# Routed attention and a Strassen MLP on one core: rows of x turned later, conversions spread anew, VectorE in written order in the first second layer

## The chip, the core and the metric

The kernel runs on one core of a Trainium2 chip. A core has TensorE (PE, matmuls, results in PSUM), VectorE (DVE), ScalarE (ACT) and GpSimd (POOL), and SyncE (SP), which issues most DMAs here. Each engine works through its own instructions in order and waits on semaphores for the others. The metric is the device time of one execution in microseconds.

## The reference, cut to what matters

Attention with 8 heads in 4 sequences of 768 tokens: a query sees only the keys that have the same nearest centroid (of 16). Then an MLP with layer norm and a residual on rows of 512. The weights come as 64-bit floats.

```python
q_assign = np.argmax(np.einsum('bhsd,hcd->bhsc', q_n, c_n), axis=-1)
k_assign = np.argmax(np.einsum('bhsd,hcd->bhsc', k_n, c_n), axis=-1)
mask = q_assign[:, :, :, None] == k_assign[:, :, None, :]
scores = scale * np.matmul(q, k.transpose(0, 1, 3, 2))
scores = np.where(mask, scores, -1000000000.0)
scores = scores - np.max(scores, axis=-1, keepdims=True)
attn = np.exp(scores)
attn = attn / (np.sum(attn, axis=-1, keepdims=True) + 1e-09)
attn_out = np.matmul(attn, v)                       # (4, 8, 768, 64)
x = attn_out.transpose(0, 2, 1, 3).reshape(4, 768, 512)
mu = np.mean(x, axis=-1, keepdims=True)
var = np.mean((x - mu) ** 2, axis=-1, keepdims=True)
xn = (x - mu) / np.sqrt(var + 1e-06) * g_ln
ch = np.maximum(xn @ w_ch1, 0.0) @ w_ch2            # 512 -> 2048 -> 512
out = x + ch
```

## The kernel before

**Attention.** Two heads of one sequence make a pair; there are 16 pairs, n = 0 to 15, four to a sequence b. In the loop over n, TensorE does in this order: `scores` for 12 blocks of keys (a mask matmul in bf16 and the f32 matmul of q and k into one bank; ScalarE then takes the exponential), the denominators `den` of pair n - 1, `weigh` for 12 blocks (exponentials times v, into `a_ps`), and `prep_sims(n + 2)`, the similarities to the centroids. The bank of `sim_ps` is the one that the first half of `weigh` uses in the next turn of the loop, so `weigh` waits until `prep_route` (VectorE, L328) has turned the similarities out of it.

VectorE does in this order: `prep_route(n + 1)`; the reciprocal of the denominators of pair n - 2 (`finish`, part 1); `turn_pair(n + 2)`, which turns the loaded q and k blocks and asks for the next ones; `add_up(n, 0)` and `add_up(n, 1)`, which sum the exponentials of each half; `finish(n - 2, 2)`, the product of attention output and `rb` (the reciprocals, which GpSimd's DMAs have spread over all rows); `finish(n - 2, 3)`, which turns the product to rows (L513) and stores them to `x_d` with four DMAs (L516); and `weight(n, 0)`, with `weight(n, 1)` in the pairs of `TWICE`. Sequences 1 to 3 also store the product itself to `xT_d`.

`weight` converts one of 32 chunks of 128 x 512 weights from 64 to 32 bits: a 512 KB load into `raw`, three VectorE instructions in `split_weight`, two in `join_weight`, then an adding DMA of GpSimd, and the load of the chunk after next into the freed buffer. The first 16 chunks are w1, the others the 16 row blocks of w2. 22 chunks are converted in the attention, the other 10 in the first layer of sequence 0 (`within` says in which unit). Rows 7 to 15 of w2 serve as tiles for exponentials until the attention ends.

In the attention the order of TensorE, VectorE, ScalarE and GpSimd is the written one (`manual_schedule`); SP's DMAs are ordered by a planner.

**MLP.** Both layers are one level of Strassen's scheme (seven products in place of eight), in the second layer of sequences 1 to 3 two levels. The first layer runs in eight units j, with seven parts each (`first_layer`, `first_units`): four matmuls to a part, ScalarE copies or VectorE adds after it, and `w1_sums(j + 1)` on VectorE. The first unit's first copy, L853, is `p1`; TensorE's third part adds to the same bank after it. In the first layer of sequence 0 the written order holds for TensorE, VectorE and ScalarE.

The second layer of sequence 0 (`second_layer`, L934) has seven parts of three token blocks. Around it VectorE makes `hidden_sums` and `w2_sum`, the norm of sequence 1 (`norm_rows` on its rows from `x_d`, two `xr` buffers; `norm_stats`; `norm_stat_rows`, which TensorE turns and SP spreads; `norm_apply`), `x_sum` and `w1_sums`. Only TensorE's order is written there; the planner orders the rest, and moved the first w2 sums ahead into the layer before. `w2_whole` stores the converted w2 to `w_all`, four DMAs to a group of four row blocks; the planner issues a group when its blocks are ready.

Rows of x from `x_d` serve the norm's statistics in all sequences, but the residual only in sequence 0. Sequences 1 to 3 take the residual from `xT_d`.

In sequences 1 to 3, SP's order is written as well. `unit_end(b, j)` does what comes after each unit, such as statistics of the next sequence.

Of the kernel before, what the change touches and what calls it, by code (L numbers as in the profile page):

```python
# [23 lines left out]
def kernel(  # L24
# [20 lines left out]
    Q = 32  # L45
# [35 lines left out]
    TWICE = (0, 1, 3, 4, 6, 8, 9)  # L81
# [370 lines left out]
    def finish(n, part):  # L452
# [26 lines left out]
        elif part == 1:  # L479
            nc.vector.reciprocal(rdens[:, n, :], rdens[:, n, :])  # L480
            row = dram.tile([2, S], F32, tag="row", name="row")
            nc.gpsimd.dma_start(
                out=row.rearrange("j (p e) -> (j p) e", e=DE), in_=rdens[:, n, :]
            )
            if n + 1 < len(pairs):
                if n + 2 < len(pairs):
                    rb = last.tile([P, S], F32, tag="rb", name="rb", bufs=1)
                else:
                    rb = last.tile([P, 2, S], F32, tag="two", name="rb", bufs=1)[:, 0]
            else:  # L490
                rb = late["all"][:, 2]
            for j in range(2):
                nc.gpsimd.dma_start(  # L493
                    out=rb[j * D : (j + 1) * D, :],
                    in_=row[j : j + 1, :].to_broadcast([D, S]),
                )
            late[n] = rb
        elif part == 2:
            a, x = xs.pop(n), late[n]
            if b:  # L500
                nc.vector.tensor_tensor(x, a, x, ALU.mult)
                nc.sync.dma_start(out=xT_d[b][pr], in_=x)
            else:
                late[n] = norm_tiles(b)[0][:, pr, :]
                nc.vector.tensor_tensor(late[n], a, x, ALU.mult)
        else:
            x = late.pop(n)

            if n + 1 < len(pairs):
                y = last.tile([P, S], F32, tag="y", name="y")  # L510
            else:
                y = late["all"][:, 0]
            nc.vector.transpose(y, x)  # L513
            for i in range(P // Q):
                m = pr * P + i * Q
                nc.sync.dma_start(  # L516
                    out=x_d[b].rearrange("t (a r) m -> r (t a) m", r=Q)[:, :, m : m + Q],
                    in_=y[i * Q : (i + 1) * Q].rearrange("r (g f) -> r g f", f=Q),
                )
# [187 lines left out]
    with tc.manual_schedule(engines=order | {mybir.EngineType.Pool}):  # L707
# [16 lines left out]
        for n in range(len(pairs)):  # L724
# [16 lines left out]
            if n + 2 < len(pairs):  # L741
                turn_pair(n + 2)
# [12 lines left out]
            add_up(n, 1)  # L755
            for i in own[:NT]:
                weigh(i)
            if nxt:
                for piece in pieces[4:]:
                    prep_mask(n + 1, *piece)  # L760
            if n > 1 and nxt:
                finish(n - 2, 2)
                finish(n - 2, 3)
            weight(n, 0)
# [55 lines left out]
    for m in range(len(convert), NWC):  # L820
        within.setdefault((1, 2, 2, 3, 4, 4, 5, 6, 6, 7)[m - len(convert)], []).append(m)
# [98 lines left out]
    def hidden_sums(c, late):  # L920

        a11, a12, a21, a22 = [hidden[r, l, c] for r in range(2) for l in range(2)]
        if late:
            nc.vector.tensor_tensor(a12, a12, a11, ALU.subtract)
            return
        s3 = place("e")[:, c]
        hidden["s3", c] = s3
        nc.vector.tensor_tensor(s3, a11, a21, ALU.subtract)
        nc.vector.tensor_tensor(a21, a21, a22, ALU.add)
        nc.vector.tensor_tensor(a11, a21, a11, ALU.subtract)  # L930
# [10 lines left out]
    def add_rows(b, r, tt, j, bank):  # L941
# [3 lines left out]
        o = early.tile([P, MH], F32, tag="o", name="o_sb", bufs=12)  # L945
# [397 lines left out]
    with tc.manual_schedule(engines={mybir.EngineType.PE}):  # L1343
# [5 lines left out]
        relu(len(summed))  # L1349
        w2_sum(st, 1)  # L1350
        w2_keep(1, st["t", 1])
        for tt in range(TH):
            second_layer(0, tt, 1, st)
            if tt == 0:
                first_layer(0, NFH - 1, 4)
                first_layer(0, NFH - 1, 3)
        relu(len(summed))
        for c in range(NFH):
            hidden_sums(c, False)
        w2_sum(st, 2)  # L1360
        norm_load(1)
        rows_load(1, 0)
        for part in (2, 5, 6, 7, 4, 3):
            for tt in range(TH):
                second_layer(0, tt, part, st)
                if part == 6 and tt == 0:
                    norm_stat_rows(1)
            if part == 2:
                for c in range(NFH):
                    hidden_sums(c, True)  # L1370
            if part == 5:
                w2_keep(2, st["t", 2])
                w2_sum(st, 3)
                w2_keep(3, st["t", 3])
            if part == 6:
                w2_sum(st, 4)
                w2_keep(4, st["t", 2])
            if part in (2, 5):
                for tt in range(TH):
                    norm_rows(1, (0 if part == 2 else TH) + tt)  # L1380
                if part == 5:
                    norm_stats(1)
            if part == 7:
                for i in range(2):
                    for c in range(NDC):
                        norm_apply(1, i, c)
                w2_whole()
            if part == 4:
                for i in range(1, 5):
                    x_sum(1, i)  # L1390
        w1_sums(1, 0)

    with tc.manual_schedule(engines=order | {mybir.EngineType.SP}):
# [4 lines left out]
        def unit_end(b, j):  # L1398
# [6 lines left out]
            if b == 1:  # L1405
                if j == 0:
# [287 lines left out]
```

## Time and profile before

| | |
|---|---|
| median of 3 runs (lowest, highest) | 915.58 us (913.34, 917.48) |
| profiled execution: its time / its span | 914.04 us / 912.3 us |
| granted TensorE clock, mean | 0.989 |
| TensorE busy | 878.1 us (96%) |
| VectorE busy | 705.6 us (77%) |
| ScalarE busy | 402.9 us (44%) |
| GpSimd busy | 77.3 us (8%) |
| attention / first layer, sequence 0 / second layer, sequence 0 | 0 to about 338 / to about 417 / to about 492 us |

Busy times are of one profiled execution. A group's row gives its count, the busy time, the mean of one instruction in ns, and the idle time of its engine just before it with what ended it. A matmul's end is modelled and matmuls overlap, so TensorE's stalls are read from one start to the next. A window's row gives its length and, for each engine, busy us and instructions, then the granted clock, the mean busy share of the DMA engines and GB/s.

### The profile page before, as it was taken

Reading aid. Unit: us, or ns where it says so; the run is one execution under the profiler, and the core shown is the slowest. Engines: PE = TensorE matmul, PEld = TensorE weight load, DVE = VectorE, ACT = ScalarE, POOL = GpSimd, SP = SyncE. Lnnn points to the kernel's source line nnn. Section 1 sums busy time; section 2 is a strip of 40 time slices with the busy share of each in tenths; the row PEclk is TensorE's granted clock in tenths of the full one; section 3 lists DMA queues with packets and bytes.
Section 4 is the critical chain, followed back from the end, with each engine's and each line's share of the span. In section 5 each row is a group of like instructions: output and inputs, shape, how many; then the busy total and the mean of one; then the engine's idle time right before and its main releaser. Section 6 shows DMA issues by size and latency. Waiting matters only on the chain.

```text
span 912.3 us, 13180 instructions
## 1 busy us (share of the span) xinstructions
PE 878.1 (96%) x4644; PEld 576.8 (63%) x4644; DVE 705.6 (77%) x1149; ACT 402.9 (44%) x739; POOL 77.3 (8%) x143
## 2 busy tenths in 40 slices
PE   8999899998999898999999999999999999999995
PEld 5444344443444344557887556997556997556995
DVE  5899898998989897879672777896655896655774
ACT  6787678897888642332001553111553111333110
POOL 1112111211212121110000000000000000000000
PEclk9999999999999998999999999999999999999998
DMA  7678788999997535886442647963234862420874
GB/s 152 119 166 146 149 166 165 203 179 187 195 182 150 163 98 158 206 228 173 162 145 87 218 150 261 359 202 96 61 83 144 293 201 73 70 98 28 271 201 94
DMA packets 250490, 147.87 MB, mean 162 GB/s; under 512 B 193568, under 2 KB 209072, under 8 KB 249392
## 3 DMA queue, kind: packets, MB, share of 16 engines
q1 hardware_dynamic: 234784, 130.75, 54.9%
q0 software_dynamic: 7776, 15.03, 8.2%
q10 hardware_dynamic: 7856, 1.16, 0.8%
q8 instruction: 39, 0.64, 0.3%
q14 instruction: 35, 0.29, 0.1%
HBM read 105.25 MB, written 33.25 MB: 152 GB/s over the span
## 4 chain that ended last, share of the span: by engine, by line
PE 59%; DMA 3%; issue 3%; DVE 2%; POOL 1%; ACT 0%; SPq 0%; POOLq 0%; DVEq 0%
PE x_ps L827 17%; PE x_ps L1117 12%; PE z_ps L827 9%; PE z_ps L1117 6%; PE x_ps L934 5%; PE y_ps L827 4%; PE y_ps L1117 3%; PE z_ps L934 2%; PE y_ps L934 1%; DMA flat<-dsb 1%; DMA raw<-in_moe_w_ch_dram 1%; DVE es L433 1%; DMA row<-rdens 0%; POOL rb L493 0%; DMA x_d<-y 0%
## 5 line engine op out<-in xcount | busy, mean ns | idle before, releaser
L396 PE MATMUL s_ps<-t,t 64*128 64x384 f32 x768 | 154.9, 483 | 0.0
L396 PEld LDWEIGHTS s_ps<-t,t 64*128 64x128 f32 x768 | 68.1, 187 | 38.4 <-issue 37.5
L1117 PE MATMUL x_ps<-lower,w 128*128 128x192 f32 x448 | 80.9, 326 | 0.9 <-DVE u L1132 0.9
L1117 PEld LDWEIGHTS x_ps<-lower,w 128*128 128x128 f32 x448 | 74.1, 190 | 2.6 <-DVE u L1132 1.5
L858 DVE TENSOR_TENSOR lower<-z_ps,u 128x384 f32<-128x384 f32 x56 | 31.0, 554 | 57.5 <-PE z_ps L827 47.1
L391 ACT ACTIVATE e<-s_ps 128x768 f32<-128x768 f32 x84 | 66.5, 813 | 6.0 <-PE s_ps L396 5.4
L391 ACT ACTIVATE w<-s_ps 128x768 f32<-128x768 f32 x80 | 64.5, 813 | 7.0 <-PE s_ps L396 6.4
L866 ACT ACTIVATE lower<-lower 128x384 f32<-128x384 f32 x88 | 45.1, 522 | 44.7 <-DVE lower L858 44.6
L408 PE MATMUL a_ps<-e,v_sb 128*64 128x384 f32 x336 | 59.3, 499 | 5.3 <-DVE sim_sb L328 5.3
L396 PE MATMUL s_ps<-mask,mask 64*128 64x384 bf16 x384 | 62.9, 323 | 1.2 <-ACT e L391 0.8
L408 PE MATMUL a_ps<-w,v_sb 128*64 128x384 f32 x320 | 56.3, 496 | 5.8 <-DVE sim_sb L328 5.8
L853 ACT COPY u<-x_ps 128x384 f32<-128x384 f32 x64 | 30.6, 479 | 69.6 <-PE x_ps L827 69.6
L853 ACT COPY p<-x_ps 128x384 f32<-128x384 f32 x32 | 15.1, 472 | 95.8 <-PE x_ps L827 89.8
L827 PE MATMUL x_ps<-xt,ws 128*128 128x384 f32 x128 | 48.1, 499 | 5.5 <-ACT p L853 4.3
L408 PEld LDWEIGHTS a_ps<-e,v_sb 128*64 128x64 f32 x336 | 24.0, 140 | 38.5 <-issue 29.2
L827 PE MATMUL z_ps<-xt,ws 128*128 128x384 f32 x128 | 47.5, 495 | 0.0
L827 PE MATMUL x_ps<-xn,ws 128*128 128x384 f32 x128 | 46.6, 487 | 0.0
L827 PE MATMUL x_ps<-xn,w 128*128 128x384 f32 x128 | 46.6, 487 | 0.0
L408 PEld LDWEIGHTS a_ps<-w,v_sb 128*64 128x64 f32 x320 | 22.9, 140 | 37.5 <-issue 27.4
L827 PE MATMUL x_ps<-xt,w 128*128 128x384 f32 x128 | 46.5, 486 | 0.0
L827 PE MATMUL z_ps<-xn,ws 128*128 128x384 f32 x128 | 46.5, 486 | 0.0
L827 PE MATMUL y_ps<-xn,w 128*128 128x384 f32 x128 | 46.5, 486 | 0.0
(225 smaller groups left out, 1657.9 us busy)
## 6 DMA issues: line engine op xcount, KB each, us to landing
w<-w_d SPq DMA_DIRECT2D x84, 256.0 KB, 3.3
raw<-in_moe_w_ch_dram SPq DMA_DIRECT2D x32, 512.0 KB, 5.2
w<-w_t SPq DMA_DIRECT2D x36, 256.0 KB, 5.3
w<-tb POOLq DMA_DIRECT2D x32, 256.0 KB, 6.3
w_d<-wt SPq DMA_DIRECT2D x7, 1024.0 KB, 4.7
w<-w_all SPq DMA_DIRECT2D x27, 256.0 KB, 3.0
v_sb<-in_v_dram SPq DMA_DIRECT2D x32, 192.0 KB, 6.7
xr<-x_d SPq DMA_DIRECT2D x24, 256.0 KB, 3.0
```

The source lines that it names most:

```text
L391: nc.scalar.activation(e, s[:, :, :HC], AF.Exp, scale=SCALE)
L396: nc.tensor.matmul(s[:, j, :HC], of_keys[:, keys], of_queries[:, o : o + HC], start=part == first, stop=part != first, skip_group_check=True,)
L408: nc.tensor.matmul(acc[j * D : (j + 1) * D, :HC], loaded[n]["v"][:, j, c, :], e[:, j, :], start=(c == 0), stop=(c == NT - 1),)
L433: nc.vector.tensor_tensor(es, e[0] if m == 1 else es, e[m], ALU.add)
L827: nc.tensor.matmul(bank[:, :HC], lhs[:, c, :], rhs[:, c], start=first and c == 0, stop=c == NDH - 1, skip_group_check=True,)
L853: nc.scalar.copy(t, bank[:, :HC])
L858: nc.vector.tensor_tensor(h, bank[:, :HC], other, ALU.add)
L866: nc.scalar.activation(h, h, AF.Relu)
L934: nc.tensor.matmul(bank[:, :MH].rearrange("p (h f) -> p h f", h=2), hidden[lhs + (c,)][:, tt * P : (tt + 1) * P], rhs[:, :, c], start=firs ...
L1117: nc.tensor.matmul(bank, w[:, c, :], a[:, c], start=way in (1, 2, 5) and c == 0, stop=c == NQH - 1, skip_group_check=True,)
```

## The change

- `LATER = 2`: for sequences 2 and 3 the attention no longer turns the product to rows; it only stores it to `xT_d`. A new `rows_out` holds the turn and the four DMAs. `columns_load` fetches such a block from `xT_d` again and `columns_turn` turns and stores it: five of the eight in the second layer of sequence 0, three in units 1, 3 and 5 of sequence 1.
- `TWICE` becomes (1, 10, 11, 12): 19 chunks are converted in the attention and 13 in the first layer of sequence 0, two in each of the units 2 to 7.
- In the attention `weight(n, 0)` stands ahead of `finish(n - 2, 2)`, and `turn_pair(2)` moves from the scores of pair 0 to behind `add_up(0, 1)`.
- In the second layer of sequence 0 VectorE's order is written too: a table `jobs` says what comes after each part and token block. `hidden_sums` is cut into three steps, and the tile `o` has 9 buffers where it had 12.

```diff
--- before.py
+++ after.py
@@ -78,7 +78,9 @@
     pairs = [(b, pr) for b in range(B) for pr in range(NPAIR)]
     loaded = {n: {} for n in range(len(pairs))}
 
-    TWICE = (0, 1, 3, 4, 6, 8, 9)
+
+    LATER = 2
+    TWICE = (1, 10, 11, 12)
 
 
     def load_blocks(n, name):
@@ -503,20 +505,34 @@
             else:
                 late[n] = norm_tiles(b)[0][:, pr, :]
                 nc.vector.tensor_tensor(late[n], a, x, ALU.mult)
+        elif b < LATER:
+            rows_out(b, pr, late.pop(n), last.tile([P, S], F32, tag="y", name="y"))
         else:
-            x = late.pop(n)
-
-            if n + 1 < len(pairs):
-                y = last.tile([P, S], F32, tag="y", name="y")
-            else:
-                y = late["all"][:, 0]
-            nc.vector.transpose(y, x)
-            for i in range(P // Q):
-                m = pr * P + i * Q
-                nc.sync.dma_start(
-                    out=x_d[b].rearrange("t (a r) m -> r (t a) m", r=Q)[:, :, m : m + Q],
-                    in_=y[i * Q : (i + 1) * Q].rearrange("r (g f) -> r g f", f=Q),
-                )
+            late.pop(n)
+
+    def rows_out(b, pr, x, y):
+
+        nc.vector.transpose(y, x)
+        for i in range(P // Q):
+            m = pr * P + i * Q
+            nc.sync.dma_start(
+                out=x_d[b].rearrange("t (a r) m -> r (t a) m", r=Q)[:, :, m : m + Q],
+                in_=y[i * Q : (i + 1) * Q].rearrange("r (g f) -> r g f", f=Q),
+            )
+
+    turning = [(b, pr) for b in range(LATER, B) for pr in range(NPAIR)]
+    asked = list(turning)
+    columns = {}
+
+    def columns_load(tile_of):
+        if asked:
+            b, pr = asked.pop(0)
+            columns[b, pr] = tile_of()
+            nc.sync.dma_start(out=columns[b, pr], in_=xT_d[b][pr])
+
+    def columns_turn(tile_of):
+        b, pr = turning.pop(0)
+        rows_out(b, pr, columns.pop((b, pr)), tile_of())
 
 
     stat_d = [spill.tile([2, S], F32, name=f"stat_d{b}") for b in range(B)]
@@ -738,7 +754,7 @@
             extras(n, "scores")
             if 1 < n and nxt:
                 finish(n - 2, 1)
-            if n + 2 < len(pairs):
+            if n and n + 2 < len(pairs):
                 turn_pair(n + 2)
             if not nxt:
                 finish(n - 1, 1)
@@ -753,15 +769,17 @@
                 for piece in pieces[:4]:
                     prep_mask(n + 1, *piece)
             add_up(n, 1)
+            if n == 0:
+                turn_pair(2)
             for i in own[:NT]:
                 weigh(i)
             if nxt:
                 for piece in pieces[4:]:
                     prep_mask(n + 1, *piece)
+            weight(n, 0)
             if n > 1 and nxt:
                 finish(n - 2, 2)
                 finish(n - 2, 3)
-            weight(n, 0)
             extras(n, "weigh")
             for i in own[NT:]:
                 weigh(i)
@@ -818,7 +836,7 @@
 
     within = {}
     for m in range(len(convert), NWC):
-        within.setdefault((1, 2, 2, 3, 4, 4, 5, 6, 6, 7)[m - len(convert)], []).append(m)
+        within.setdefault((1, 2, 2, 3, 3, 4, 4, 5, 5, 6, 6, 7, 7)[m - len(convert)], []).append(m)
     MH = DM // 2
     hidden = {}
 
@@ -917,17 +935,18 @@
             cs = slice(c, c + 2)
             nc.vector.tensor_tensor(o[:, :, cs], x[:, :, cs], y[:, :, cs], ALU.subtract)
 
-    def hidden_sums(c, late):
-
-        a11, a12, a21, a22 = [hidden[r, l, c] for r in range(2) for l in range(2)]
-        if late:
-            nc.vector.tensor_tensor(a12, a12, a11, ALU.subtract)
-            return
-        s3 = place("e")[:, c]
-        hidden["s3", c] = s3
-        nc.vector.tensor_tensor(s3, a11, a21, ALU.subtract)
-        nc.vector.tensor_tensor(a21, a21, a22, ALU.add)
-        nc.vector.tensor_tensor(a11, a21, a11, ALU.subtract)
+    def hidden_sums(i, chunks):
+
+        for c in chunks:
+            a11, a12, a21, a22 = [hidden[r, l, c] for r in range(2) for l in range(2)]
+            if i == 1:
+                s3 = hidden["s3", c] = place("e")[:, c]
+                nc.vector.tensor_tensor(s3, a11, a21, ALU.subtract)
+                nc.vector.tensor_tensor(a21, a21, a22, ALU.add)
+            elif i == 2:
+                nc.vector.tensor_tensor(a11, a21, a11, ALU.subtract)
+            else:
+                nc.vector.tensor_tensor(a12, a12, a11, ALU.subtract)
 
     def second_product(bank, tt, lhs, rhs, first):
         for c in range(NFH):
@@ -942,7 +961,7 @@
 
         x = early.tile([P, MH], F32, tag="xb", name="xb", bufs=4)
         nc.sync.dma_start(out=x, in_=x_d[b][r * TH + tt, :, j * MH : (j + 1) * MH])
-        o = early.tile([P, MH], F32, tag="o", name="o_sb", bufs=12)
+        o = early.tile([P, MH], F32, tag="o", name="o_sb", bufs=9)
         nc.vector.tensor_tensor(o, bank[:, :MH], x, ALU.add)
         return o
 
@@ -1340,55 +1359,66 @@
                 for part in ((1,), (2, 3))[j // 2]:
                     finish(len(pairs) - 1, part)
 
-    with tc.manual_schedule(engines={mybir.EngineType.PE}):
+    with tc.manual_schedule(engines={mybir.EngineType.PE, mybir.EngineType.DVE}):
         st = {}
         rest.close()
         ffn = pool("ffn", 2)
         fifth.append(ffn.tile([P, NFH, HC], F32, name="fifth", bufs=1))
         early = first.enter_context(tc.tile_pool(name="early", bufs=1))
         relu(len(summed))
+        norm_load(1)
+        rows_load(1, 0)
+
+        def column():
+            return early.tile([P, S], F32, tag="col", name="col", bufs=2)
+
+        def turn_columns():
+            columns_turn(lambda: early.tile([P, S], F32, tag="turned", name="turned", bufs=1))
+            if len(turning) > 4:
+                columns_load(column)
+
+        def keep(i, t):
+            return lambda: w2_keep(i, st["t", t])
+
+        def do(f, *args):
+            return lambda: f(*args)
+
         w2_sum(st, 1)
         w2_keep(1, st["t", 1])
-        for tt in range(TH):
-            second_layer(0, tt, 1, st)
-            if tt == 0:
-                first_layer(0, NFH - 1, 4)
-                first_layer(0, NFH - 1, 3)
-        relu(len(summed))
-        for c in range(NFH):
-            hidden_sums(c, False)
-        w2_sum(st, 2)
-        norm_load(1)
-        rows_load(1, 0)
-        for part in (2, 5, 6, 7, 4, 3):
+        jobs = {
+            (1, 0): [
+                do(first_layer, 0, NFH - 1, 4), do(first_layer, 0, NFH - 1, 3), do(relu, 1),
+                do(hidden_sums, 1, range(3)),
+            ],
+            (1, 1): [do(hidden_sums, 1, range(3, NFH - 1))],
+            (1, 2): [do(hidden_sums, 1, range(NFH - 1, NFH)), do(w2_sum, st, 2), keep(2, 2)],
+            (2, 0): [do(hidden_sums, 2, range(3))],
+            (2, 1): [do(hidden_sums, 2, range(3, NFH))],
+            (2, 2): [do(norm_rows, 1, 0), do(norm_rows, 1, 1), do(hidden_sums, 4, range(2))],
+            (5, 0): [
+                do(columns_load, column), do(norm_rows, 1, 2), do(norm_rows, 1, 3),
+                do(hidden_sums, 4, range(2, 5)),
+            ],
+            (5, 1): [do(columns_load, column), do(norm_rows, 1, 4), do(norm_rows, 1, 5), do(norm_stats, 1)],
+            (5, 2): [do(hidden_sums, 4, range(5, NFH)), turn_columns],
+            (6, 0): [do(norm_stat_rows, 1), do(w2_sum, st, 3), keep(3, 3)],
+            (6, 1): [turn_columns],
+            (6, 2): [do(w2_sum, st, 4), keep(4, 2)],
+            (7, 0): [turn_columns, do(norm_apply, 1, 0, 0), do(norm_apply, 1, 0, 1)],
+            (7, 1): [do(norm_apply, 1, 0, 2), do(norm_apply, 1, 0, 3)],
+            (7, 2): [turn_columns, do(norm_apply, 1, 1, 0), w2_whole],
+            (4, 0): [do(norm_apply, 1, 1, 1), do(norm_apply, 1, 1, 2)],
+            (4, 1): [turn_columns, do(norm_apply, 1, 1, 3)],
+            (4, 2): [do(x_sum, 1, 1), do(x_sum, 1, 2)],
+            (3, 0): [do(x_sum, 1, 3)],
+            (3, 1): [do(x_sum, 1, 4), do(w1_sums, 1, 0)],
+            (3, 2): [],
+        }
+        for part in (1, 2, 5, 6, 7, 4, 3):
             for tt in range(TH):
                 second_layer(0, tt, part, st)
-                if part == 6 and tt == 0:
-                    norm_stat_rows(1)
-            if part == 2:
-                for c in range(NFH):
-                    hidden_sums(c, True)
-            if part == 5:
-                w2_keep(2, st["t", 2])
-                w2_sum(st, 3)
-                w2_keep(3, st["t", 3])
-            if part == 6:
-                w2_sum(st, 4)
-                w2_keep(4, st["t", 2])
-            if part in (2, 5):
-                for tt in range(TH):
-                    norm_rows(1, (0 if part == 2 else TH) + tt)
-                if part == 5:
-                    norm_stats(1)
-            if part == 7:
-                for i in range(2):
-                    for c in range(NDC):
-                        norm_apply(1, i, c)
-                w2_whole()
-            if part == 4:
-                for i in range(1, 5):
-                    x_sum(1, i)
-        w1_sums(1, 0)
+                for job in jobs[part, tt]:
+                    job()
 
     with tc.manual_schedule(engines=order | {mybir.EngineType.SP}):
         first.close()
@@ -1403,6 +1433,13 @@
                 if j < NT:
                     norm_rows(b + 1, j)
             if b == 1:
+                def row():
+                    return xpool.tile([P, S], F32, tag="row", name="col", bufs=2)
+
+                if turning and j % 2:
+                    columns_turn(row)
+                elif asked and j % 2 == 0:
+                    columns_load(row)
                 if j == 0:
                     outer["ends"] = all_in_range()
                 if j == 2:
```

## The prediction

> **What bounds the kernel now.** I read the page's engine rows first, then the list of waits, then a table of windows cut at pairs and stages, then the timelines of TensorE, ScalarE and VectorE at the few places where TensorE starts late.
>
> ```profile
> PE 878.1 (96%) x4644; PEld 576.8 (63%) x4644; DVE 705.6 (77%) x1149; ACT 402.9 (44%) x739; POOL 77.3 (8%) x143
> ```
>
> TensorE is busy for 878.1 of 912.3 us, so about 34 us are all that work on other engines can give, and some of that is start-up. The waits say where those microseconds lie (total, times, longest):
>
> ```profile
> PE a_ps L408 <- DVE sim_sb L328: 14.0, 7, 3.3
> PE x_ps L827 <- ACT p L853: 4.3, 1, 4.3
> DVE ta L263 <- DMA raw<-in_moe_w_ch_dram: 7.2, 2, 5.7
> DVE xn L505 <- DMA rb<-row: 6.1, 4, 2.1
> DVE rb L501 <- DMA rb<-row: 5.4, 5, 1.8
> DVE xn L599 <- DMA stat_row<-stat_d: 3.1, 2, 2.9
> ```
>
> Seven times TensorE stands before `weigh`, because its PSUM bank still holds the similarities until VectorE turns them (L328). VectorE is simply late. The windows, from one L328 to the next, show why (us, then busy of PE, PEld, DVE, ACT, POOL, clock, DMA share, GB/s):
>
> ```profile
> 79.91:102.71 22.80, 20.51 (x148) 9.15 (x144) 20.12 (x28) 17.13 (x25) 4.54 (x7) 1.00 0.78 138
> 205.17:227.81 22.64, 19.32 (x136) 9.01 (x136) 20.10 (x28) 17.08 (x28) 4.55 (x7) 1.00 0.93 186
> 246.38:266.07 19.69, 19.69 (x140) 8.98 (x136) 17.31 (x23) 17.47 (x28) 3.64 (x6) 1.00 0.91 166
> 354.40:417.20 62.80, 61.58 (x192) 36.09 (x191) 50.92 (x109) 22.13 (x48) 10.37 (x14) 1.00 0.77 199
> 417.20:492.30 75.10, 75.10 (x346) 65.16 (x346) 47.37 (x94) 3.86 (x7) 0.00 (x0) 1.00 0.44 149
> ```
>
> TensorE's own time for a pair is 19.25 us (`den` starts at 246.91 and at 266.16, nothing idle between). A pair with one weight chunk converted costs VectorE 17.3 us and fits; one with two costs 20.1 us plus 1.2 to 2.1 us of waiting for `rb`, and doesn't. The first second layer (last row) has no idle TensorE at all. What a long stall costs beyond itself:
>
> ```profile
> 99.57 0.85 PE L464 MATMUL den_ps<-two,ones 128*32 128x384 f32 x8
> 103.34 2.14 PE L408 MATMUL a_ps<-once,v_sb 128*64 128x384 f32 x8 [2.92 <-DVE sim_sb L328]
> ```
>
> After it eight matmuls span 2.14 us instead of the 1.51 after a short stall: the clock has fallen to half for five starts (0.64 apart instead of 0.32). The MLP's start, on three engines:
>
> ```profile
> 344.52 0.48 ACT L853 COPY p<-x_ps 128x384 f32<-128x384 f32 x1 [5.97 <-DMA x_d<-y]
> ```
> ```profile
> 345.05 2.93 PE L827 MATMUL x_ps<-xt,ws 128*128 128x384 f32 x4 [4.28 <-ACT p L853]
> ```
> ```profile
> 340.42 0.98 DVE L513 STREAM_TRANSPOSE y<-rb 128x768 f32<-128x768 f32 x1
> 341.32 0.92 DVE L433 TENSOR_TENSOR es<-e 128x768 f32<-128x768 f32 x1
> 342.34 2.02 DVE L433 TENSOR_TENSOR es<-es,once 128x768 f32<-128x768 f32 x2
> ```
>
> The profile names a transfer for ScalarE's wait, but `p` of the pool `hid` takes over memory of the tile `once`, whose last readers are the two adds that end at 344.36, 0.16 us before `p` starts. So this too is VectorE being late.
>
> **The change part by part.** The sum is against the profiled execution, 914.04 us (span 912.3); the median shown is 915.58, 1.5 higher.
>
> *Stalls of pairs, removed.* From `den` to the first `a_ps` takes 0.78 us unstalled (61.07 to 61.85). The seven stalled ones, start to start less 0.78: at 40.4 1.39, at 99.6 2.99, at 123.5 1.44, at 163.8 1.51, at 203.8 1.20, at 224.3 3.39, at 305.1 2.61; sum 14.5. Slow clock after those at 99.6 and 305.1: five starts by 0.30, 1.5 each, 3.0. At 318.4 `den` waits 0.7 for a late sum. Together 18.2. Why they should go: `TWICE` now holds pairs 1, 10, 11, 12. Pair 1 has no `rb` and no turn yet (18 us). Pairs 10 to 12 finish pairs 8 to 10, whose turn (0.98, 0.90 from start to start) and four `x_d` issues (2.2 us of SP) have left: 20.1 - 0.9 = 19.2, level with TensorE. Nothing else has two chunks. And the conversion now stands ahead of the product with `rb`. From the reciprocal to the arrival of `rb` takes about 12.3 us (268.4 to 280.65), while VectorE's work between was 10.8 (two turns 1.9, two `add_up` 4.5 each); with the chunk's 2.7 it is 13.5, so the `rb` waits (11.5 in all) should go. Behind the product stand only the store of xT_d on SP and, for b < 2, the turn; both come 2.7 later, with a pair's time to spare. VectorE can then run ahead: after the last exponential it needs 0.9 + 4.5 + 2.7 + 1.0 + 1.0, about 10 us, to reach a L328 due at 19.9. That lead, up to 9 us, lasts through pairs 10 to 12 at 5 to 7 us.
>
> *`turn_pair(2)` moved behind `add_up(0, 1)`.* It no longer waits for its loads (3.66 and 2.34 us at 23.3 and 26.6). But its two turns end at about 19.6 + 4.5 + 4.5 + 1.9 = 30.5, and TensorE wants them at 29.85 (`sim_ps`): +0.65.
>
> *Statistics of sequence 0.* `norm_apply` waited 2.94 us at 306.1, since SP put the `stat_row` loads (300.93) behind the xT_d store. That store comes later now; SP's order is a planner's, so the loads may go ahead of it. If they do, the wait is 0; if not, they land some 5.5 us after the store and the lead is used up. Bounds 0 and 6; I take 0.5, nearer the first, because in time of readiness they come first.
>
> *Start of the MLP.* Counted from the first `weigh` of pair 15 (T, now 330.03), the reciprocal of pair 14 waits for a transfer chain until about T - 2.3, then add_up(15,0) 5.1, x sums and w1 sums 4.2, product 1.0, no turn (-0.9), and `es` starts at T + 8.0; TensorE resumes 3.7 later (341.32 to 345.05), T + 11.7, and would be ready at T + 10.6. So a stall of about 1.2 takes the place of 4.4, and the slow clock after it (0.48 and seven times 0.32, 2.7) goes: -6.0; bounds -7.1 and 0.
>
> Here a rule meets the trace. The Trainium skill, "TensorE: Matmul & The Clock Gate", "Why this matters for your kernels", has the clock drop after TensorE gaps of more than about 3 us. Here gaps of 2.92, 2.53 and 4.28 were followed by half clock, one of 3.31 was not. By the rule the gaps of 3.31 and 4.28 alone would carry a penalty (about 3.4 in all, at half of its 3.4 us window each); measured, it is 1.5 + 1.5 + 2.7 = 5.7. I take the trace's.
>
> *First layer of sequence 0, 13 chunks instead of 10.* A unit is 28 matmuls at 0.3225, 9.03 us. With two chunks VectorE has 5.4 + three sums 1.5 + w1 sums 1.5 = 8.4: it fits, but all of units 2 to 7 have two now. What doesn't surely fit is the loads. A raw buffer is wanted again 5.6 to 6.1 us after it is free; landings took 3.7 to 9.0 (median 4.4), and twice SP issued one 1.3 and 2.7 late, behind four `w_all` stores. The group of `w_all` at 307.7 moves into this stage as well, since row 3 of w2 is now converted here. Three such collisions of 2.5 to 3 are 8 us of VectorE waits; about 4 are absorbed (w1 sums are ready 3 us early), so 3.9 of stall instead of the 1.4 at 410: +2.5. In favour: the early w2 sums (2.7 on VectorE) and their 1 MB store at 397.96, ahead of the 9.03 landing, leave for the written order. Bounds -1.4 and +9.
>
> *Second layer in written order, five turns in it, three in sequence 1.* TensorE's time is unchanged. VectorE has 47.4 + 2.5 + five turns 4.9 = 55 of 75 us; in sequence 1's units 1, 3, 5 0.98 each beside 4.5 to 5 idle per 20. Five loads and twenty 128-byte-packet stores (3072 packets, 2.2 us of the 16 engines a pair) join a stage at DMA share 0.44. The tightest places I find in order are the y bank at part 2 (about 2 us early) and TensorE's transpose of sequence 1's statistics behind part 6: six rows through two buffers end at about 35.6 us into the layer, wanted at 37.1. +0.5; bounds 0 and 4, were loads later by 2 each. `o` with 9 buffers is hidden: 12 tiles, the first three stored two parts before the tenth.
>
> Sum: 914.0 - 18.2 + 0.65 + 0.5 - 6.0 + 2.5 + 0.5 = 894.0; at the level of the median, 895.
>
> **The rivals.** *VectorE's lead doesn't form* (0.17): stat_row stays behind the store, or `rb` grows later with the chunk's traffic. The two-chunk stalls still go by arithmetic, but 3 to 4 stay in pairs 10 to 13 and the MLP start keeps its 7: 914 - 18.2 + 4 + 0.65 + 3 = 903.5, or 905 by the median. For it: the 2.94 wait; against: the missing SP stores.
>
> *The stalls move into the first layer* (0.15): raw loads bind, +9 instead of +2.5: 900.5, or 902. For it: the 5.72 us that VectorE waited at 407.7; against: a DMA share of 0.77 there, from which the `x_d` stores of two pairs leave.
>
> *The written order holds up TensorE* (0.10), the slower case. In the second layer VectorE can't step past a late row any more. Rows 2 to 5 of sequence 1 are three round trips of a two-buffer load (3 us each) that SP issues in an order not written out; behind a late row stand w2 sum 3, the bank adds and the statistics, and TensorE's transpose waits for them. SP has stood 13.4 us before one such row load. With 1.5 us to spare, the gain of 20 is gone once each trip is 7 longer; at 10 each, 28.5 is lost: 923. Against it: the DMA engines are half idle there.
>
> *It does nothing* (0.06): another cause keeps L328 late, such as exponentials; ScalarE's 17.5 of 19.25 leaves little for that.
>
> **How the numbers follow.** The forecast has 0.52, its own range 886 to 900. With the two middle rivals the range is 886 to 907; the slower case and half of "nothing" lie above. This kernel can tell 0.5% from no change, 911.0 to 920.2: faster 0.85, same 0.06, slower 0.09. Predicted 895.
>
> **What would show it.** Right: `a_ps <- sim_sb` near 0, `den` starts 19.25 apart throughout, L501 and L505 without waits, clock rows at full through the pairs, the step at the MLP's start about 1 us, some raw waits in 360 to 400. Wrong: L328 still within 1 us of `den`; `stat_row` waits of 3 or more; TensorE idle before `stat_ps` or `y_ps` in the second layer; raw waits above 10 us.

## The result, and the profile after

The changed kernel takes 904.73 us (median of 4 runs, 902.43 to 906.89); in the same comparison the kernel before takes 916.53 (913.34 to 918.20). The ratio is 0.9875, with a 95% interval of 0.9837 to 0.9913. The forecast was 895 with a range of 886 to 907. The direction and that range hold, but of about 20 us of gain only some 12 came, and the main forecast's own range, 886 to 900, was missed. The wider range holds because it took in two rivals; one of them, the stalls that move into the first layer (902), is what happened. The profiled execution of after took 904.72 us, 9.3 less than that of before (914.04); the sums below are made in it.

The page's engine row and the waits of TensorE in after (total, times, longest, in us):

```profile
PE 876.6 (97%) x4644; PEld 575.4 (64%) x4644; DVE 704.5 (78%) x1149; ACT 402.8 (45%) x739; POOL 77.4 (9%) x143
```
```profile
PE x_ps L845 <- DVE ws L658: 4.3, 3, 2.5
PE x_ps L845 <- ACT u L871: 2.7, 1, 2.7
PE x_ps L953 <- DVE o_sb L965: 2.4, 1, 2.4
...
PE x_ps L845 <- ACT p L871: 0.8, 1, 0.8
```

The row that led the list before, seven waits of `a_ps` for `sim_sb` with 14.0 us, is gone: no `a_ps` stands in the list. What leads now is the MLP: the weight sums (L658), a copy `u` (L871) and the adding of the second layer's rows (L965). What VectorE itself waits for says why:

```profile
DVE ta L265 <- DMA raw<-in_moe_w_ch_dram: 14.1, 4, 6.7
...
DVE o_sb L965 <- DMA xb<-x_d: 6.2, 1, 6.2
DVE two L445 <- ACT w L393: 6.0, 4, 1.8
```

The waits for raw weights have doubled (7.2 before), one wait for `xb` is new, and no wait for `rb` is left anywhere in it. Instead VectorE now waits for ScalarE's exponentials (L445), which is what an engine with a lead does. How far it leads: in after, VectorE turns a pair's similarities (L330) at 185.63, 9.05 us ahead of `den` at 194.68.

```profile
185.63 0.54 DVE L330 STREAM_TRANSPOSE sim_sb<-sim_ps 128x384 f32<-128x384 f32 x1
```
```profile
194.68 0.85 PE L466 MATMUL den_ps<-two,ones 128*32 128x384 f32 x8
```

Over the pairs the lead is 4.7 to 9.1 us. The windows, from one `den` to the next for three pairs, then by stage (us, busy of PE, PEld, DVE, ACT, POOL, clock, DMA share, GB/s):

```profile
79.17:98.42 19.25, 19.25 (x138) 8.99 (x136) 18.70 (x22) 15.27 (x23) 4.54 (x8) 1.00 0.88 162
194.68:213.94 19.26, 19.26 (x139) 9.00 (x137) 17.30 (x21) 16.94 (x28) 3.63 (x6) 1.00 0.87 179
252.44:271.90 19.46, 19.46 (x140) 9.07 (x138) 18.94 (x28) 17.99 (x27) 4.55 (x7) 1.00 0.93 181
330.00:400.00 70.00, 65.60 (x201) 38.27 (x199) 50.73 (x108) 21.41 (x46) 11.05 (x14) 0.98 0.80 224
400.00:475.00 75.00, 68.91 (x306) 58.29 (x306) 52.30 (x102) 4.79 (x9) 1.74 (x2) 0.98 0.66 185
```

The pairs run at TensorE's own 19.25 us with nothing idle. In the first layer (fourth row) TensorE is idle for 4.4 us, in the last row, the end of the first layer and the second, for 6.1: before, the second layer lacked nothing. The three longest places, in TensorE's timeline of after (start, length, and the idle time before it with what ended it):

```profile
360.90 2.90 PE L845 MATMUL x_ps<-xt,ws 128*128 128x384 f32 x4 [2.52 <-DVE ws L658]
...
404.61 2.70 PE L845 MATMUL x_ps<-xt,w 128*128 128x384 f32 x4 [2.73 <-ACT u L871]
```
```profile
463.42 4.80 PE L953 MATMUL x_ps<-w2t,lower 128*128 128x256 f32 x21 [2.35 <-DVE o_sb L965]
```

The first two also pay in clock: four matmuls span 2.90 and 2.70 us, where four unslowed ones, 0.3225 apart, span 1.45. On VectorE these three stalls begin as waits for a transfer:

```profile
353.75 0.43 DVE L265 TENSOR_SCALAR ta<-raw 128x512 uint32<-128x512 uint32 x1 [6.70 <-DMA raw<-in_moe_w_ch_dram]
```
```profile
398.49 0.43 DVE L265 TENSOR_SCALAR ta<-raw 128x512 uint32<-128x512 uint32 x1 [5.74 <-DMA raw<-in_moe_w_ch_dram]
```
```profile
462.94 0.42 DVE L965 TENSOR_TENSOR o_sb<-x_ps,xb 128x256 f32<-128x256 f32 x1 [6.20 <-DMA xb<-x_d]
```

And in front of each of these loads SP's queue shows a group of stores (start, time for the group, number issued):

```profile
341.62 3.17 SPq L1044 DMA_DIRECT2D w_all<-w  x4
344.89 15.42 SPq L252 DMA_DIRECT2D raw<-in_moe_w_ch_dram  x4
```
```profile
388.89 3.32 SPq L1044 DMA_DIRECT2D w_all<-w  x4
392.31 1.99 SPq L252 DMA_DIRECT2D raw<-in_moe_w_ch_dram  x2
```
```profile
455.06 3.54 SPq L518 DMA_DIRECT2D x_d<-turned  x4
...
459.21 4.50 SPq L963 DMA_DIRECT2D xb<-x_d  x5
```

The raw load issued at 344.89 landed at 353.73, 8.84 us later; the one issued at 336.54, with no such group ahead of it, took 3.74. VectorE had read the buffer empty at 342.04, so the load also went out 2.8 us late. The four issues alone (3.2 us) don't explain that: SP had come to the group at 336.92 and first stood 4.7 us, until GpSimd's adding DMA had written the weights that the first store reads.

```profile
SPq L1044 <- DMA w<-tb: 4.7, 1, 4.7
```

So such a group can take twice: the load is issued late, and it is longer on the way. At the second group the parts differ: the load at 392.31 was 4.6 us late and took 6.2 to land.

### The profile page after: what moved, and what is told of

Read it like the earlier page. It is cut to its first block, busy times and chain, and to the rows that moved or that the text cites. A ratio compares the mean times of both kernels' runs of the same rounds, so it can differ in the third digit from the quotient of the medians.

```text
span 902.8 us, 13188 instructions
## 1 busy us (share of the span) xinstructions
PE 876.6 (97%) x4644; PEld 575.4 (64%) x4644; DVE 704.5 (78%) x1149; ACT 402.8 (45%) x739; POOL 77.4 (9%) x143
## 4 chain that ended last, share of the span: by engine, by line
PE 81%; DVE 7%; DMA 7%; SPq 2%; issue 2%; ACT 1%; DVEq 0%; ACTq 0%; POOLq 0%
PE s_ps L398 16%; PE x_ps L845 13%; PE a_ps L410 13%; PE x_ps L1136 12%; PE z_ps L845 7%; PE z_ps L1136 6%; PE y_ps L845 3%; DMA raw<-in_moe_w_ch_dram 3%; PE y_ps L1136 3%; PE x_ps L953 2%; PE den_ps L466 1%; PE sim_ps L317 1%; PE y_ps L953 1%; PE z_ps L953 1%; DVE lower L876 1%
## 5 line engine op out<-in xcount | busy, mean ns | idle before, releaser
L871 ACT COPY u<-x_ps 128x384 f32<-128x384 f32 x64 | 30.5, 477 | 64.6 <-PE x_ps L845 64.6
L871 ACT COPY p<-x_ps 128x384 f32<-128x384 f32 x32 | 15.1, 471 | 94.1 <-PE x_ps L845 91.6
```

What stands on the lines that cost most here:

```text
L871: nc.scalar.copy(t, bank[:, :HC])
```

## Experiments

Ten kernels were run, in three sets, each set on one chip with its own runs of the kernel before (medians 915.57, 916.75 and 917.91 us). None leaves anything out.

**The order in the attention alone.** The kernel before with one move:

```diff
+            weight(n, 0)
             if n > 1 and nxt:
                 finish(n - 2, 2)
                 finish(n - 2, 3)
-            weight(n, 0)
```

> The kernel before with one edit: weight(n, 0) ahead of finish(n - 2, 2). Theory A (the waits for rb, 11.5 us in all, were what kept VectorE from ever running ahead; with them gone a two-chunk pair of 20.1 us is paid from the lead of the one-chunk pairs): pair stalls fall from 14.5 us plus 3.0 of slow clock to about 3 to 5 (pair 0 and its 1.4 stay, pairs 3 and 4 in a row leave 1 to 2), time 903 to 907. Theory B (the places of the two-chunk pairs are what matters, 20.1 against 19.25): stalls of about 0.9 in each of the seven pairs stay at least, with MLP start 7: time 910 to 915.

Measured: 900.85 us, ratio 0.9844 (0.9814 to 0.9875). This is better than Theory A's 903 to 907, and the single move is at least as good as the whole change (0.9875). The waits of VectorE for `rb`, 11.5 us before, then those of TensorE:

```profile
DVE rb L501 <- DMA rb<-row: 0.7, 1, 0.7
```

```profile
PE a_ps L408 <- DVE sim_sb L328: 4.7, 5, 1.4
PE x_ps L827 <- ACT p L853: 3.9, 1, 3.9
PE den_ps L464 <- DVE two L447: 2.3, 1, 2.3
```

The 14.0 us of `a_ps` fall to 4.7, and the granted clock stays full behind all of them. The lead itself stays small here: L328 starts between 1.6 us after `den` and 3.9 ahead of it. The 8 us with which after and the run with 22 chunks begin (at `den` of 40.7) come with the second chunk taken from pair 0 and `turn_pair(2)` moved; the runs don't separate these two. The MLP's start keeps its 3.9, with the turns still in the attention; the run below that moves only the rows has 0.7 there. This kernel's second layer has no idle TensorE.

**Order and conversions, the rows left in the attention.** The kernel before with that move, the new `TWICE` and `within`, and `turn_pair(2)` moved; second layer as before:

```diff
-    TWICE = (0, 1, 3, 4, 6, 8, 9)
+    TWICE = (1, 10, 11, 12)
```

> The kernel before with all edits of the attention's VectorE order and of the conversions (order, TWICE, within, turn_pair(2)), but rows of all sequences turned in the attention and the second layer left to the planner. Theory A (lead alone pays for pairs 10 to 12): no pair stalls although their turns stay; first layer of sequence 0 loses as the changed kernel does (raw loads), nothing is lost inside the second layer: time 902 to 906, level with the changed kernel. Theory B (moving the rows is needed for the pairs and for the MLP's start): 0.9 of stall in each of pairs 10 to 13 and 4 to 7 at the MLP's start: 910 to 914.

Measured: 914.38 us, ratio 0.9982 (0.9959 to 1.0005), no gain at all. Theory A missed; the time comes out close to Theory B's, but not by its reasons. Its pairs do run at 19.25 us up to 291 us, turns and all: so the turns need not leave for the pairs to be even. The time is lost behind them:

```profile
DVE ta L263 <- DMA raw<-in_moe_w_ch_dram: 15.1, 6, 5.7
...
DVE xn L599 <- DMA stat_row<-stat_d: 7.1, 1, 7.1
```
```profile
PE x_ps L829 <- ACT p L855: 4.2, 1, 4.2
PE a_ps L408 <- DVE sim_sb L328: 3.2, 1, 3.2
PE x_ps L829 <- ACT u L855: 3.1, 1, 3.1
PE y_ps L936 <- DVE o_sb L960: 2.7, 1, 2.7
PE z_ps L829 <- DVE lower L860: 2.5, 1, 2.5
```

Two of my unknowns are seen here at their bad ends. `stat_row` comes 7.1 us late and costs TensorE 3.2 plus slow clock at 292 us; and thirteen chunks in the first layer make VectorE wait six times for raw weights.

**The group of `w_all` out of the first layer.** The changed kernel, `w2_whole` put off to units 0 to 3 of sequence 1, a group of four stores each. It is written behind part 7 of the second layer, but SP's order there is a planner's, and its stores had come forward into the first layer:

```diff
-    def w2_whole():
+    def w2_whole(group):
...
-            (7, 2): [turn_columns, do(norm_apply, 1, 1, 0), w2_whole],
+            (7, 2): [turn_columns, do(norm_apply, 1, 1, 0)],
...
+                if j < 4:
+                    w2_whole(j)
```

> The changed kernel, with the w_all stores (w2_whole) put off to units 0 to 3 of sequence 1, one group of four DMAs each. Theory C (raw loads come late in the first layer because SP stands before a w_all store that waits for an adding DMA, and because that group's transfers run ahead of the load): the VectorE waits of 6.7 and 5.7 us for raw fall under 2, the stalls of 4.4, 1.7 and 6.2 us in first layer and second layer's start fall to 2 or 3 in sum: time 893 to 898. Theory D (two chunks a unit are too many for VectorE and the DMA engines in any order): waits for raw stay at 4 or more, time 901 to 906.

Measured: 896.32 us, ratio 0.9787 (0.9756 to 0.9818). The conversions are as in the change, and the first layer, then the wait for raw weights:

```profile
330.00:400.00 70.00, 70.00 (x228) 43.12 (x228) 59.77 (x127) 25.21 (x53) 12.83 (x16) 1.00 0.80 207
```
```profile
DVE ta L265 <- DMA raw<-in_moe_w_ch_dram: 0.6, 1, 0.6
```

As Theory C had it, TensorE is busy throughout, and 14.1 us of waits are 0.6. The mean DMA share is 0.80 as in the changed kernel, so it was not the traffic of the whole stage but the group ahead of the load. Its fourth load of raw weights in this stretch:

```profile
343.12 0.33 SPq L252 DMA_DIRECT2D raw<-in_moe_w_ch_dram  x1
```

It comes 5.52 us after the third one (337.60) and lands 4.89 later; in after it came 8.35 behind the third (336.54) and landed 8.84 later. The difference, 2.8 of issue and 4.0 on the way, is the 6.70 that VectorE waited. The mean over 70 us hides how full the DMA engines are in just those microseconds (second last column; first the load's flight in after, then here):

```profile
344.89:353.73 8.84, 8.84 (x29) 5.19 (x28) 2.13 (x6) 2.76 (x6) 0.88 (x1) 1.00 1.02 275
```
```profile
343.12:348.01 4.89, 4.89 (x17) 2.90 (x16) 4.82 (x11) 1.16 (x3) 2.75 (x4) 1.00 0.83 200
```

Whether the load waited for its place in the queue or for its share of full engines isn't separated: removing the group removes both. The stalls of 6.8 and 6.2 are gone, 13.0 in all; the profiled time falls by 8.4 only, because the stall at `xb` is longer here by 1.8 with its slow clock, and sequence 1, where the stores now are, lacks 1.9 more, which leaves 0.9 open.

**22 chunks in the attention instead of 19.** The changed kernel, three conversions taken back out of the first layer, `within` as before:

```diff
-    TWICE = (1, 10, 11, 12)
+    TWICE = (1, 4, 6, 8, 10, 11, 12)
```

> The changed kernel with 22 chunks in the attention again (TWICE = 1, 4, 6, 8, 10, 11, 12) and the old ten in the first layer. Theory A (VectorE's lead of up to 9 us pays for more two-chunk pairs): pairs keep 19.25 us, first layer and second layer's start lose 1 to 3 instead of 13: time 892 to 897. Theory B (19 was as much as the attention can take): stalls come back at pairs 9 to 13, 1 to 3 us each, and the MLP's start is late by 4 to 7: 900 to 907.

Measured: 893.00 us, ratio 0.9754 (0.9722 to 0.9786), inside Theory A's range. `den` still comes every 19.25 us, and the first layer is full, though the `w_all` groups are back in it; one raw wait of 4.1 is absorbed:

```profile
330.00:400.00 70.00, 70.00 (x229) 43.23 (x228) 52.45 (x112) 25.30 (x53) 10.24 (x13) 1.00 0.78 212
400.00:475.00 75.00, 72.87 (x323) 61.95 (x322) 52.12 (x99) 2.04 (x5) 0.00 (x0) 0.98 0.63 173
```

So the attention did not need the relief of three chunks: VectorE's lead, 8 us at first and 5 to 7.5 here after that, pays for seven pairs with two chunks, three of them (10 to 12) in a row. The three chunks cost in the first layer what they were spared for in the attention.

**The parts of the change taken back one by one.** First the written order of VectorE in the second layer: only TensorE's order is written, the rest is the change.

```diff
-    with tc.manual_schedule(engines={mybir.EngineType.PE, mybir.EngineType.DVE}):
+    with tc.manual_schedule(engines={mybir.EngineType.PE}):
```

> The changed kernel, with VectorE's order in the second layer of sequence 0 left to the planner (TensorE's alone is written). Theory G (written order costs: VectorE stands 6.2 us before one add): the stall of 2.5 at part 7 goes, the ones before it stay: 901 to 903. Rival H (written order costs nothing, SP's order does): xb is behind the turned stores here too, 904 to 907; were the planner to bring the turns ahead of adds that free TensorE's banks, slower than the changed kernel, 907 to 915.

Measured: 904.44 us, ratio 0.9878 (0.9827 to 0.9929), level with the change and inside H's range, though not by H's reason. The stall at `xb` is gone, and the waits for raw weights are 4.3 us where after has 14.1; but the planner makes a new stall. It hoists a turn of the second layer into the first, where VectorE stands before it:

```profile
336.40 0.98 DVE L515 STREAM_TRANSPOSE turned<-col 128x768 f32<-128x768 f32 x1 [10.86 <-DMA col<-xT_d]
```

TensorE then lacks 8.5 us at 330 to 339, with 1.9 of slow clock behind it. Gains and losses cancel, so the run doesn't tell what the written order costs by itself; it shows what it prevents, a moved turn ahead of work that TensorE needs.

Second, the attention as before (order, `TWICE`, `within`, `turn_pair`), with the moved rows and the written second layer kept:

> The changed kernel with the attention's VectorE order, TWICE, within and turn_pair(2) as in the kernel before: only the rows are moved and the second layer written out. Theory A (order is what paid in the pairs): pair stalls stay at 12 to 15 us with slow clock 1.5 to 3, the MLP's start gains 3 to 7, the second layer loses 2.5 to 4 and sequence 1 1.5: 911 to 915. Theory B (moving the rows relieves VectorE enough by itself): 904 to 908.

Measured: 910.61 us (10 runs), ratio 0.9927 (0.9899 to 0.9955), just under Theory A's range. The pairs' stalls are there again (one row below), about 14 us with their slow clock, while the first layer, with its ten chunks, has one stall of 2.0 where after has 13 us in the first layer and at the start of the second.

```profile
PE a_ps L410 <- DVE sim_sb L330: 10.2, 7, 3.0
```

Moving the rows out of the attention doesn't even it; the order does. The profiled difference to after, 3.6, is what these terms give: 14.0 of pairs more, 11.0 of the first layer and the second's start less, 0.8 of `sim_ps` less: 2.2, which leaves 1.4 unexplained.

**The second layer's wait for `xb`.** In the kernel with 22 chunks I put the stores of the second layer's turned rows on ScalarE's queue:

```diff
-            nc.sync.dma_start(
+            queue.dma_start(
...
+        rows_out(b, pr, columns.pop((b, pr)), tile_of(), queue)
```

> The kernel of the run with 22 chunks (893.0 us), with one edit: in the second layer of sequence 0 the four stores of each turned block are issued by ScalarE's queue instead of SP's. Theory E (xb stands in SP's queue behind stores that wait for VectorE's turn, and VectorE's written order lets nothing pass the add that waits for xb): the wait of 5.8 us for xb goes, and with it TensorE's stall of 2.3 with 1.7 of slow clock: 888.5 to 890. Theory F (the transfers themselves are late, since small packets fill the DMA engines): xb lands as late as before, 892 to 894.

Measured: 896.54 us, ratio 0.9781 (0.9733 to 0.9830): missed. The `xb` stall did go, and no wait for `xb` is left, so the stores in SP's queue were its cause. But at sequence 1's first unit a new one came, 5.1 us and 2.9 of slow clock:

```profile
473.52 2.90 PE L845 MATMUL x_ps<-xt,ws 128*128 128x384 f32 x4 [5.08 <-DVE ws L658]
```
```profile
468.55 0.56 DVE L876 TENSOR_TENSOR lower<-y_ps,p 128x384 f32<-128x384 f32 x1 [7.92 <-PE y_ps L845]
```

The edit touched only the queue, yet the planner has put this add of the next stage ahead of x sums and w1 sums that TensorE's part 6, the third in that unit, needs; VectorE stands 7.92 us before it. ScalarE's queue, too, stood 21.6 us at twelve of the stores, waits included. It doesn't show that ScalarE's queue is bad for these stores; it shows that the plan can move another engine's work.

The same kernel with two more edits, `turn_pair(2)` between the two `add_up` of pair 0, and sequence 1's turns behind its loads for w2:

> The kernel with 22 chunks and stores on ScalarE's queue, and two more edits: turn_pair(2) between the two add_up of pair 0, and in sequence 1 the turns and column loads at the end of a unit's extra work, behind w2_split and w2_back. If the stall of 0.76 before the third sim_ps comes from turn_pair(2) ending at 30.2, and that of 1.4 to 1.7 in the last unit of sequence 1 from w2_back standing behind the stores in SP's queue, both go: 886 to 888.5. If these stalls have other causes (loads of q; DMA engines shared with the ring), 888.5 to 891.

Measured: 897.98 us (6 runs), ratio 0.9798 (0.9761 to 0.9836): missed as well, with the same 5.1 us at 473. Of its two own edits one works: the `sim_ps` stall at 29 us is gone. The other harms: at 551 TensorE lacks 2.8, where the others lack 1.4, and half clock follows.

**The good edit alone, and two buffers.** Back on SP's queue: the kernel with 22 chunks and `turn_pair(2)` between the adds, and then the same with two `turned` tiles (and six `o_sb`).

```diff
             add_up(n, 0)
+            if n == 0:
+                turn_pair(2)
             extras(n, "sums")
```

> The variant with 22 chunks (893.0) with one thing moved: the two turns of pair 2 between the two adds of pair 0's exponentials instead of behind the second. It keeps one sim_ps stall of 0.76 at 29.1, and where the turns were tried between the adds that stall was absent. If TensorE waits there only for the turned inputs: 893.0 - 0.8 = 892.2. If the adds behind the turns then make den late: 893 or a little over. The stall of 2.3 + 1.7 us at 448 (second layer, add_rows waiting for xb) and the one of 1.4 at 543.6 should stay.

Measured: 891.28 us, ratio 0.9709 (0.9685 to 0.9733): near the 892.2 expected, and the best kernel here, level with the next one. No `sim_ps` stall, no stall at the MLP's start in its profiled execution; the stall at 447 us (1.6, this time without half clock behind it) and the one at 540 (1.4) remain.

> The same, and the second layer's `turned` tile gets two buffers (o_sb six instead of nine, to make room); all stores stay on SP's queue. Theory: SP's queue stands because the store of a turned tile waits for its transpose, the transpose waits for the store before it (one buffer), and xb's loads are queued behind. With two buffers the transposes run on, so the stall of 2.3 us and the 1.7 us of slow clock behind it go: 892.2 - 4.0 = 888 (887 to 890). Rival: the stores' own length on the queue (16 times 24 pieces of 128 bytes a row) keeps xb late whatever the buffers: 892, the stall at 448 as before. Second rival: six o_sb are too few and add_rows waits for the output stores: over 893, with waits of o_sb on out_dram in the trace.

Measured: 891.41 us, ratio 0.9704 (0.9678 to 0.9730): the theory of the single buffer falls. The turns no longer wait, and `xb` comes later still:

```profile
438.58 0.97 DVE L515 STREAM_TRANSPOSE turned<-col 128x768 f32<-128x768 f32 x1
...
450.09 0.42 DVE L965 TENSOR_TENSOR o_sb<-x_ps,xb 128x256 f32<-128x256 f32 x1 [8.83 <-DMA xb<-x_d]
```
```profile
440.45 5.45 SPq L518 DMA_DIRECT2D x_d<-turned  x4
445.95 0.53 SPq L531 DMA_DIRECT2D col<-xT_d  x1
446.51 4.34 SPq L963 DMA_DIRECT2D xb<-x_d  x5
```

The four stores take SP 5.45 us, 1.1 to 1.5 each, even though the turned tile is ready at 439.56; the DMA engines are busy for 0.96 of that time. It is the stores' own time in the queue that makes `xb` late, the rival that the expectation named. A load of `xb` placed ahead of the stores was not tried.

## Why the forecast was right and where it was short

The steps, by TensorE's stalls from start to start and the slow clock behind them, forecast and measured:

| step | forecast | measured |
|---|---|---|
| stalls of pairs | -18.2 | -18.2: none is left |
| `turn_pair(2)` | +0.65 | +0.76 at 29.0 |
| `stat_row` | +0.5 | 0 |
| MLP start | -6.0 | -6.2: 0.97 is left of 4.4 and 2.7 |
| first layer, 13 chunks | +2.5 | +5.4: 6.8 instead of 1.4 |
| second layer and its start | +0.5 | +8.7: 6.2 at the start, 2.5 for `xb` |
| sequence 1 | 0 | +1.4: `y_ps` at 554.3 |
| sum | -20.05 | -8.1; the profiled times differ by 9.3 |

The attention came out as worked: the lead of VectorE formed (4.7 to 9.1 us, 7.0 to 7.4 behind pairs 10 to 12), both `rb` waits left, and the MLP's start lost its slow clock, `es` starting at T + 7.8 and TensorE resuming at T + 11.55, forecast 8.0 and 11.7. What I had wrong in it is the share of the parts. I credited the stalls to three things together (fewer chunks, no turns, the order); the runs show that the order alone takes most of it (`a_ps` 4.7 of 14.0 us left), that turns may stay for the pairs' sake, and that 22 chunks fit. That `stat_row` cost nothing is luck in part: SP's order is the planner's, and in the run with the rows left it cost 3.2 us and a stretch of half clock.

**The term that failed is the first layer's +2.5, and with it the second layer's +0.5.** The mechanism was named in the prediction, raw loads behind `w_all` stores, and the rival "the stalls move into the first layer" priced it at +9 in all; measured it is +11.6 (5.4, and 6.2 at the start of the second layer). The prediction counted three collisions at 2.5 to 3 us each, SP's delay alone. Two of them cost VectorE 6.7 and 5.7 us, with the longer landing in it; the one between (365.0 to 369.7) cost it 0.2. At the first, 4.0 are absorbed and 2.7 left on TensorE; at the second 1.7 are absorbed, and stalls of 1.2 and 2.9 left. Half clock follows 2.7 and 2.9, and the prediction had put no slow clock into this term. The last collision, at 388.9, hits the last chunks, whose stall falls behind the border that I had drawn between the stages: I had priced the second layer without what the first layer hands on to it. One run takes away the groups and one the three chunks, and either removes both stalls: the cause needs both.

The early w2 sums did not leave for the written order as I had put in favour: VectorE's L936 still stands in the first layer at 369.1 and waits 1.78 us for the store of `late`, ahead of the stall of 1.75 there. And the second layer's own stall is not the statistics' transpose or the `y` bank, the tight places I had named, but `xb`: I had counted the new stores' share of the DMA engines (2.2 us a pair) and not that on SP's queue they stand ahead of a load that VectorE needs next. The slower rival, a late row that holds TensorE's transpose of the statistics, didn't happen.

## What to carry to other kernels

When work is moved out of a crowded stage, price it where it arrives, and by queue position as much as by engine time: the conversions fitted VectorE in the first layer to within a few per cent, yet a group of stores ahead of their load cost 6 to 7 us at two of three places. Ask first which single part of a change removes the stalls; here two swapped calls gave as much as the whole change, and the whole change with 22 chunks in the attention about twice as much. A stall of TensorE is worth more than its length wherever the clock falls behind it, so the longest are cut first.

## What the runs showed of the hardware that I had not expected

A load of 512 KB behind four stores of 256 KB on one queue took 8.84 us to land, and 4.89 without them, though the mean DMA share of the stage was 0.80 both times; within the load's flight it was 1.02 against 0.83. A mean over a stage doesn't show such a crowd.

Four stores of a turned tile, in pieces of 128 bytes, keep SP 2.1 to 5.5 us in five kernels (after, `w_all` put off, 22 chunks, and the last two). Those over 3.4 us all fell where the DMA share was 0.81 or more; at 0.68 or less it was 2.1 to 3.3.

The length of a gap doesn't say by itself whether TensorE's clock falls. In the kernel with 22 chunks and in the one with only the rows moved, TensorE is idle 2.13 us at the same add for `xb`; half clock follows in the first and not in the second. The prediction noted the same: gaps of 2.53 and 2.92 us were followed by half clock, one of 3.31 was not. The traces show what differs. Within a trace the changes of the granted clock lie whole multiples of 3.413 us apart (in before at 104.08, 107.50, 308.88, 312.30, 343.02 and 349.84), at other places in each run. Cut at these points, the two gaps look like this (us, PE busy, and the clock as third last number; 22 chunks first):

```profile
448.14:451.55 3.41, 1.28 (x6) 0.81 (x5) 1.18 (x3) 0.00 (x0) 0.00 (x0) 1.00 0.73 242
451.55:454.96 3.41, 3.41 (x9) 2.70 (x8) 3.38 (x6) 0.00 (x0) 0.00 (x0) 0.50 0.33 110
```
```profile
463.27:466.68 3.41, 1.48 (x7) 0.95 (x5) 0.28 (x1) 0.00 (x0) 0.00 (x0) 1.00 0.90 258
466.68:470.09 3.41, 3.21 (x15) 2.86 (x16) 3.34 (x7) 0.00 (x0) 0.00 (x0) 1.00 0.32 100
```

In the first the whole gap, 2.13 us, lies in one window of 3.41; in the second it is cut into 1.93 and 0.20. In all twelve traces, start-up and end left out, half clock followed each of the 17 full-clock windows with 2.13 us or more of idle TensorE and none with 1.94 or less; between these two nothing was measured. It lasted one window in 12 cases and two in 5. The gap of 3.31 us in before was cut into 1.84 and 1.48. So whether a gap between about 2.1 and 3.9 us (twice 1.94, an estimate) costs half clock depends on where it falls, and the slow clock in these sums, forecast and measured, belongs to the profiled executions.
